# Retention and a gated MLP on one Trainium2 core: a weight load issued one instruction earlier, and a store and a load moved behind a later attention visit

## The chip, the core and the metric

The kernel runs on one core of a Trainium2 chip. The core has a matrix engine (TensorE; PE in the profile, with its weight loads as PEld), a vector engine (VectorE, DVE), a scalar engine (ScalarE, ACT), a general engine (GpSimd, POOL) and a sync engine (SyncE, SP) that issues transfers. Each runs its own list of instructions in order and waits on semaphores for the others. Transfers run on 16 DMA engines; those that POOL issues, and that change the type on the way, go by the software queue, those that SP issues by the hardware queues. The metric is the device time of one launch in microseconds (us): 291.16 us before, the median of 3 runs (291.06 to 291.24).

## The reference

Eight batches of eight heads, 576 positions, head size 64: scores masked by a decay that depends on the head and the distance, times v (no softmax). Its output, 4608 tokens of 512, goes through a two-layer MLP whose activation is h cos(h).

```python
scores = scale * np.matmul(q, k.transpose(0, 1, 3, 2))
Dmat = np.where(rel >= 0, gamma[:, None, None] ** rel[None, :, :], 0.0)
out = np.matmul(scores * Dmat[None], v)
x = np.ascontiguousarray(out.transpose(0, 2, 1, 3)).reshape(B * S, H * D)
h = x @ w_in                      # 512 -> 2048
return (h * np.cos(h)) @ w_out    # 2048 -> 512
```

## The kernel before

**Tiling.** Tokens are handled in 18 blocks of 256 (index j) for the attention and in 9 tiles of 512 (index n, two blocks each) for the MLP. The decay gamma^(i-j) is split into a factor for q's position and one for k's, so q and k are scaled row by row (`scaled`, L192: one instruction for each half y of a block), transposed by the matrix engine, multiplied to scores, masked (L312, L341), and multiplied by v (`out_own`, L433). What came earlier in a sequence enters by running state sums (`sums_of`, L351) and `out_carried` (L478), whose last matmul is kept as `tiles["end"]`. The result is cast to x, the first matrix's input. `mm1` (L520, matmuls at L534) makes h in eight groups a tile; ACT takes the cosine, DVE multiplies (L547, L548). `mm2_seven` (L670) makes the second product of a tile as seven products of half size, numbered x, in the order 1, 2, 6, 4, 7, 5, 3; their sums are the tile's four output quarters c11, c21, c22 and u1.

**The order.** The instructions of each engine stand in the order in which the program text emits them. In the opening (L899 to L948) the attention of blocks 0 and 1 is written out by hand between the loads of the weights. `load_w_in(e0, part)` (L812) has POOL issue a load of 512 columns of w_in; `part` 0 or 1 is the first or second half of the contraction. So w_in's first 512 columns come as piece one, `load_w_in(0, 0)`, and piece two, `load_w_in(0, 1)`; the next 512 as pieces three and four. The first group of h multiplies piece one for all its four parts, then block 1's attention output comes in between (`block1_outputs`, L979, with the casts of x at L984), then it multiplies piece two. Block 1's k is scaled by POOL in two halves (L920, L922), its q by DVE in two halves (L927); twelve transposes (L928 to L930, at L260) follow in the order q half 0, k half 1, q half 1, each group of four with its copy out of PSUM (L265) by DVE, ACT and DVE. POOL's casts of v (`round_v`, L933) and the other weight pieces follow.

**Later attention.** From the third tile on, two blocks' attention is visited between products: in the third tile (n = 2), a first visit ahead of product 7 (`mid_unit`, L1152) and a second ahead of product 3 (`end_unit`, L1165). Both call `outputs`, which ends with `out_carried` and so sets `tiles["end"]`.

**SP's queue.** SP issues all loads of q, k, v (`load`, L133; three buffers for each) and the stores of the outputs (`stored_rows`, L659, two DMAs for each quarter) in order. `store(...)` in `mm2_seven` decides when a finished quarter goes out; `late[x]` holds what is emitted right behind the visit ahead of product x. `gate=` makes the first DMA of a call wait for an instruction. The branch for n = 2 and the first quarter (s = 0, c11) is the one that changes. `loaded` is the next block to load; there it is 11.

Of the kernel before, what the change touches and what calls it, by code (L numbers as in the profile page):

```python
# [17 lines left out]
def kernel(  # L18
# [75 lines left out]
    tiles = {}  # L94
# [23 lines left out]
    def parts_of(t0, n, per):  # L118

        cut = -t0 % S  # L120
        if 0 < cut < n:
            return [(0, cut // per, t0), (cut // per, n // per, t0 + cut)]
        return [(0, n // per, t0)]
# [9 lines left out]
    def load(j, names="qkv", gate=None):  # L133
        for name in names:
            src = {"q": q, "k": k, "v": v}[name]
            if name == "q" or j < NP_B:
                f = ld.tile([P, H, 2, D], F32, tag="f" + name, name=f"f{name}")
                for p0, p1, t in parts_of(j * BK, BK, 2):
                    b, s0 = divmod(t, S)
                    i = nc.sync.dma_start(  # L140
                        f[p0:p1].rearrange("p h r d -> p h (r d)"),
                        src[b, :, s0 : s0 + 2 * (p1 - p0), :].rearrange(
                            "h (p r) d -> p h (r d)", r=2
                        ),
                    )
                    if gate is not None:
                        after(i, gate)
                        gate = None
            else:
                f = ld.tile([P, 2, H, D], F32, tag="f" + name, name=f"f{name}")  # L150
                for y in range(2):
                    for p0, p1, t in parts_of(j * BK + y * P, P, 1):
                        b, s0 = divmod(t, S)
                        i = nc.sync.dma_start(
                            f[p0:p1, y],
                            src[b, :, s0 : s0 + p1 - p0, :].rearrange("h s d -> s h d"),
                        )
                        if gate is not None:
                            after(i, gate)
                            gate = None  # L160
            tiles["f" + name, j] = f
        return i
# [90 lines left out]
    def transpose_pe(j, name, bank, evac, ys=(0, 1)):  # L253
        if ("qkT", j) not in tiles:
            new_qkT(j)
        m = "qk".index(name)
        ps = psum.tile([P, len(ys), HG, P], BF16, tag=bank, name="tr")
        for u, y in enumerate(ys):
            for hg in range(HG):
                nc.tensor.transpose(  # L260
                    ps[:, u, hg, :],
                    tiles["qks", j][:, m, y, hg].rearrange("s a d -> s (a d)"),
                    ident,
                )
        evac(tiles["qkT", j][:, m, ys[0] : ys[-1] + 1], ps)  # L265
# [404 lines left out]
    def mm2_seven(n, at, stored, xs=(1, 2, 6, 4, 7, 5, 3), early=None):  # L670
        pend = []

        def flush():
            while pend:
                pend.pop(0)()

        def add(out_, in0, in1):
            return lambda: nc.vector.tensor_tensor(out=out_, in0=in0, in1=in1, op=ALU.add)  # L678

        def copied(tag, x):  # L680
            t = op.tile([P, 2, N2], F32, tag=tag, name="ot")
            held.append(lambda ps=tiles["all", x]: nc.scalar.copy(t, ps))  # L682
            return t

        late = {4: [], 7: [], 3: []}

        def store(t, r, c, s):
            where = n * W + r * 256, c * N2, (c + 1) * N2, t

            def go():  # L690
                nonlocal loaded
                if 2 < n < last and s == 0:
                    stored_rows(*where, halves=(0,))
                    late[4].append(lambda: stored_rows(*where, halves=(1,), gate=tiles["end"]))
                    stored(s, late)
                elif n == 2 and s == 0:
                    step(False)

                    def behind(j=loaded):
                        stored_rows(*where, gate=tiles["end"])  # L700
                        load(j, "q")

                    late[7].append(behind)
                    late[3].append(lambda j=loaded: load(j, "kv", gate=tiles["end"]))
                    loaded += 1
                elif 1 < n < last - 1 and s == 1:
                    late[3].append(lambda: stored_rows(*where))
                else:
                    queues = (nc.sync, nc.scalar) if n == last and s else (nc.sync, nc.sync)
                    stored_rows(*where, queues)  # L710
                    stored(s)

            return go

        def copies():
            while held:
                held.pop(0)()

        for x in xs:
            if x not in at:  # L720
                copies()
                flush()
            else:
                if at[x].__name__ in ("nothing", "first_scores", "last_outputs", "turning"):
                    copies()
                at[x](flush, pend)
                copies()
                for run in late.pop(x, ()):
                    run()
            if x == 6 and n > 1:  # L730
                late_sums(n, (3,))
            parts = product(n, x, early)
            if x == 1:
                c11 = copied("a", 1)
                tiles["c11"] = c11
                if n > 1:
                    late_sums(n, (5, 6))
            elif x == 2:
                c11 = tiles["c11"]
                if n == 1:  # L740
                    p2 = copied("d", 2)
                    continue
                pend[:0] = [add(c11, c11, tiles["all", 2]), store(c11, 0, 0, 0)]
            elif x == 6:
                u1 = copied("b", 1)
            elif x == 4:
                c21 = copied("c", 4)
            elif x == 7 and n == 1:
                pend += [
                    add(c21, c21, tiles["all", 1]),  # L750
                    add(c22, c22, tiles["all", 1]),
                    store(c21, 1, 0, 1),
                    store(c22, 1, 1, 2),
                ]
            elif x == 7:
                c22 = copied("d", 1)
                pend += [add(c21, c21, tiles["all", 1]), store(c21, 1, 0, 1)]
            elif x == 5 and n == 1:
                c22 = copied("d", 5)
            elif x == 5 and n == last:  # L760
                for (j, c0, c1), ps in zip(parts, tiles["o", 5]):
                    pend.append(add(c22[:, j, c0:c1], ps, c22[:, j, c0:c1]))
                pend.append(store(c22, 1, 1, 2))
            elif x == 5:
                pend += [
                    add(c22, c22, tiles["all", 5]),
                    add(u1, u1, tiles["all", 5]),
                    store(c22, 1, 1, 2),
                ]
            elif n < last:  # L770
                pend += [add(u1, u1, tiles["all", 5 if n == 1 else 3]), store(u1, 0, 1, 3)]
                if n == 1:
                    pend += [add(c11, c11, p2), store(c11, 0, 0, 0)]
                flush()
            else:
                flush()
                copies()
                for (j, c0, c1), ps in zip(parts, tiles["o", 5]):
                    add(u1[:, j, c0:c1], ps, u1[:, j, c0:c1])()
                    if c1 == N2:  # L780
                        stored_rows(
                            n * W + j * P, N2, DM, u1[:, j : j + 1, :], (nc.sync, nc.scalar)
                        )

    loaded, prepared = 2, 0
# [26 lines left out]
    def load_w_in(e0, part=None):  # L812
        dgs = slice(0, DG) if part is None else slice(2 * part, 2 * part + 2)
        return nc.gpsimd.dma_start(  # L814
            w_in_sb[:, dgs, e0 : e0 + 512],
            moe_w_in[:, e0 : e0 + 512].rearrange("(dg p) e -> p dg e", p=P)[:, dgs],
        )
# [97 lines left out]
    w_dma = [load_w_in(0, 0)]  # L915
# [3 lines left out]
    sums_of(0, "st")()()  # L919
    scaled(nc.gpsimd, 1, "k", 0)  # L920
    transpose_pe(1, "k", "b", act, (0,))
    scaled(nc.gpsimd, 1, "k", 1)  # L922
    w_dma += [load_w_in(0, 1), load_w_in(512, 0)]
    ps0 = psum.tile([P, DG, BK], F32, tag="m", name="ov")
    out_own(0, ps0)
    for y in range(2):
# [287 lines left out]
```

## Time and profile before

| what | value |
|---|---|
| median of 3 runs | 291.16 us (291.06 to 291.24) |
| the profiled execution's own time | 291.54 us |
| its span, first to last instruction | 289.8 us |
| granted clock of the matrix engine, mean | 0.997 |
| chain that ended last: share of PE, of DMA | 92%, 4% |
| PE waiting for the load of w_in at L534 | 0.2 us, once |
| POOL waiting for the loads of v (L214), of k, of q (L203) | 6.8, 5.7 and 3.1 us |
| first group of h, first half; second half and all that follows | from 14.83; from 17.54 us |
| third tile: products from, to (fourth tile's h from) | 95.92, 111.86 us |

The span is what the profile covers; the time of a run has what lies around it too. Times inside the span count from its start. A row of the timeline merges neighbours of one line and form: start, length, engine, line, operation, out<-in, shapes, count, and in brackets the idle time before it and what ended it.

### The profile page before, as it was taken

How to read it: one execution, taken by the hardware profiler on the slowest of the kernel's cores; microseconds unless marked ns; L12 is line 12 of the kernel's file. 1: busy time of each engine (PE TensorE's matmuls, PEld its weight loads, DVE VectorE, ACT ScalarE, POOL GpSimd, SP SyncE). 2: the span in 40 equal slices, each digit the busy share in tenths (PEclk: the TensorE clock that was granted, in tenths of full speed). 3: DMA queues.
4: the chain of work that ended last, by engine and by line, in shares of the span. 5: the costliest groups of instructions: out<-in, count | busy, mean ns of one | idle time of the engine just before them, and what ended most of it. 6: DMA issues, size and time to landing. Idle time of an engine off the chain costs nothing.

```text
span 289.8 us, 10531 instructions
## 1 busy us (share of the span) xinstructions
PE 283.2 (98%) x4336; PEld 190.3 (66%) x4336; DVE 217.7 (75%) x311; ACT 169.5 (58%) x200; POOL 146.0 (50%) x169
## 2 busy tenths in 40 slices
PE   7999999999999999999999999999999999999994
PEld 2664446888844786478646874687458845874584
DVE  5767769969967977796789677977698669745943
ACT  6756316755677655677467747673767376536620
POOL 7940524786996993379236933594348023002300
PEclk9999999999999999999999999999999999999998
DMA  7999999997897897783883289317501120122013
GB/s 219 271 178 203 237 218 239 232 228 187 212 223 190 209 242 181 193 215 98 185 225 80 53 212 240 86 43 186 141 0 41 48 67 0 36 60 56 0 38 109
DMA packets 103853, 42.62 MB, mean 147 GB/s; under 512 B 68480, under 2 KB 103296, under 8 KB 103808
## 3 DMA queue, kind: packets, MB, share of 16 engines
q1 hardware_dynamic: 99104, 37.37, 52.6%
q0 software_dynamic: 4256, 4.19, 9.1%
q8 instruction: 36, 0.59, 0.9%
q10 hardware_dynamic: 448, 0.39, 0.4%
q14 instruction: 9, 0.07, 0.1%
HBM read 36.70 MB, written 9.44 MB: 159 GB/s over the span
## 4 chain that ended last, share of the span: by engine, by line
PE 92%; DMA 4%; POOL 1%; SPq 0%; issue 0%; ACT 0%; DVE 0%; POOLq 0%
PE h L534 43%; PE o L649 35%; PE o L1069 5%; PE tr L239 3%; PE ov L449 2%; DMA w_in_sb<-in_moe_w_in_dram 2%; DMA fv<-in_v_dram 2%; PE sc L332 2%; PE ov L484 1%; PE st L365 1%; POOL qks L203 1%; SPq L140 0%; POOL w_in_sb L814 0%; POOL vb L214 0%; ACT ot L682 0%
## 5 line engine op out<-in xcount | busy, mean ns | idle before, releaser
L534 PE MATMUL h<-xT,w_in_sb 128*128 128x512 bf16 (+1 forms) x656 | 127.8, 353 | 0.2 <-DMA w_in_sb<-in_moe_w_in_dram 0.2
L548 DVE TENSOR_TENSOR gT<-h,cosh 128x1024 bf16<-128x1024 f32 x72 | 87.8, 1221 | 28.2 <-ACT cosh L547 27.2
L547 ACT ACTIVATE cosh<-h,half_pi 128x1024 f32<-128x1024 f32 x72 | 80.1, 1114 | 39.5 <-PE h L534 39.5
L534 PEld LDWEIGHTS <-w_in_sb 128*128 128x128 bf16 x656 | 63.4, 98 | 59.3 <-issue 1.0
L588 POOL TENSOR_TENSOR gs<-gT 128x512 bf16<-128x512 bf16 x30 | 38.1, 1270 | 99.2 <-DVE gT L548 97.2
L649 PEld LDWEIGHTS <-gs 128*128 128x128 bf16 x528 | 49.6, 98 | 5.9
L203 POOL TENSOR_TENSOR qks<-fk,gkc 128x512 bf16<-128x512 f32 x32 | 38.5, 1222 | 5.7 <-DMA fk<-in_k_dram 5.7
L649 PEld LDWEIGHTS <-gT 128*128 128x128 bf16 x384 | 36.6, 98 | 6.1
L678 DVE TENSOR_TENSOR ot<-ot,o 128x512 f32<-128x512 f32 x35 | 23.3, 682 | 21.0 <-ACT ot L682 11.0
L245 ACT COPY qkT<-tr 128x1024 bf16<-128x1024 bf16 x28 | 26.8, 1022 | 13.0 <-PE tr L239 11.0
L203 POOL TENSOR_TENSOR qks<-fq,gq 128x512 bf16<-128x512 f32 x28 | 30.6, 1111 | 5.4 <-DMA fq<-in_q_dram 3.1
L649 PE MATMUL o<-w_out_sb,gs 128*128 128x256 bf16 (+1 forms) x264 | 30.7, 270 | 0.0
L649 PE MATMUL o<-w_out_sb,gT 128*128 128x256 bf16 x256 | 30.6, 273 | 0.0
L649 PE MATMUL o<-ws,gs 128*128 128x256 bf16 (+1 forms) x264 | 30.4, 269 | 0.0
L682 ACT COPY ot<-o 128x512 f32<-128x512 f32 x33 | 19.3, 584 | 19.1 <-PE o L649 19.1
L341 DVE TENSOR_TENSOR ret<-sc,mask_c 128x512 bf16<-128x512 f32 x32 | 20.6, 682 | 6.4 <-PE sc L332 6.4
L214 POOL CAST vb<-fv 128x512 bf16<-128x512 f32 x35 | 20.9, 621 | 6.9 <-DMA fv<-in_v_dram 6.8
L425 ACT CAST sb<-s_all 128x768 bf16<-128x768 f32 (+2 forms) x17 | 15.6, 919 | 14.6 <-DVE s_all L416 14.4
L416 DVE TENSOR_TENSOR s_all<-st,s_all 128x256 f32<-128x256 f32 x49 | 20.6, 421 | 1.4
L505 ACT CAST xT<-ov 128x1024 bf16<-128x1024 f32 (+1 forms) x16 | 15.2, 959 | 7.5 <-PE ov L484 7.4
L588 DVE TENSOR_TENSOR gs<-gT 128x512 bf16<-128x512 bf16 (+1 forms) x24 | 15.7, 654 | 0.5
L649 PE MATMUL o<-ws,gT 128*128 128x256 bf16 x128 | 15.3, 273 | 0.0
(85 smaller groups left out, 211.8 us busy)
## 6 DMA issues: line engine op xcount, KB each, us to landing
out_dram<-ot SPq DMA_DIRECT2D x68, 128.0 KB, 2.7
fk<-in_k_dram SPq DMA_DIRECT2D x28, 256.0 KB, 4.6
fv<-in_v_dram SPq DMA_DIRECT2D x28, 256.0 KB, 5.0
fq<-in_q_dram SPq DMA_DIRECT2D x12, 512.0 KB, 5.8
w_out_sb<-in_moe_w_out_dram POOLq DMA_DIRECT2D x4, 512.0 KB, 9.8
fq<-in_q_dram SPq DMA_DIRECT2D x4, 384.0 KB, 5.5
fk<-in_k_dram SPq DMA_DIRECT2D x2, 512.0 KB, 6.0
fv<-in_v_dram SPq DMA_DIRECT2D x2, 512.0 KB, 5.9
```

What stands on the lines that cost most here:

```text
L203: return eng.tensor_tensor(out=dst.rearrange("p b a d -> p a b d"), in0=src.rearrange("p (a b) d -> p a b d", a=2), in1=by.rearrange("p (a ...
L214: runs[y](vb[:, y], f[:, :, y, :] if j < NP_B else f[:, y])
L245: lambda r=r: evacs[r](tiles["qkT", j][:, :, :, :, r * HP : r * HP + HP], pss[r])
L341: nc.vector.tensor_tensor(out=ret[:, he].rearrange("p b y i -> p (b y) i"), in0=ps[he].rearrange("p b y i -> p (b y) i"), in1=mask_c.unsqu ...
L416: nc.vector.tensor_tensor(out=s32[:, u], in0=ps[c.half][:, c.y], in1=s32[:, u - 1] if u else tiles["run"], op=ALU.add,)
L534: nc.tensor.matmul(ps[:, j, :], lhsT=w_in_sb[:, dg, (et + j) * P : (et + j + 1) * P], rhs=xT[:, dg, c0 : c0 + w], start=dg == 0 and not (i ...
L547: nc.scalar.activation(cosh, ps, ACTF.Sin, bias=half_pi, scale=1.0)
L548: nc.vector.tensor_mul(gT[:, et : et + m, c0 : c0 + w], ps, cosh)
L588: i = eng.tensor_tensor(out=tiles["gs", n, x][:, e : e + step], in0=a[:, e : e + step], in1=b[:, e : e + step], op=op_,)
L649: nc.tensor.matmul(dst[i], lhsT=lhs[:, e, j * P : (j + 1) * P], rhs=rhs[:, e, c0:c1], start=(fresh and e == 0 and (i == 0 or len(parts) > 2)),
L678: return lambda: nc.vector.tensor_tensor(out=out_, in0=in0, in1=in1, op=ALU.add)
L682: held.append(lambda ps=tiles["all", x]: nc.scalar.copy(t, ps))
```

## The change

In the opening, the issue of piece two moves up by one instruction of POOL: between the two halves of block 1's k instead of behind both. Piece three stays behind the second half, and the list `w_dma`, by which later loads are gated, keeps its order.

In the third tile, the store of c11 and the load of q of block 11, so far emitted behind the visit ahead of product 7 (the store gated on that visit's last carried matmul), and the load of k and v, emitted behind the visit ahead of product 3 and gated on that one, become one step behind the visit ahead of product 3: store, gated on that visit's last carried matmul, then q, k and v. `load(j)` without names loads q, k, v in this order, without a gate of its own. SP's list there was: c11's two stores, q (two DMAs), c22's two stores, k (three), v (three), c21's stores. It becomes: c22's two stores, c11's two stores, q, k, v, c21's stores. The lists of the matrix, vector and scalar engines stay as they are.

```diff
-        late = {4: [], 7: [], 3: []}
+        late = {4: [], 3: []}
...
                     def behind(j=loaded):
                         stored_rows(*where, gate=tiles["end"])
-                        load(j, "q")
-
-                    late[7].append(behind)
-                    late[3].append(lambda j=loaded: load(j, "kv", gate=tiles["end"]))
+                        load(j)
+
+                    late[3].append(behind)
                     loaded += 1
...
     scaled(nc.gpsimd, 1, "k", 0)
     transpose_pe(1, "k", "b", act, (0,))
+    w_dma.append(load_w_in(0, 1))
     scaled(nc.gpsimd, 1, "k", 1)
-    w_dma += [load_w_in(0, 1), load_w_in(512, 0)]
+    w_dma.append(load_w_in(512, 0))
```

## The prediction

> **What bounds the kernel now.** I read the page's busy shares first, then the chain of waits, then the timeline of the opening, then single instructions where DVE and POOL meet, then SP's queue in the third tile.
>
> The page and the chain:
>
> ```profile
> PE 283.2 (98%) x4336; PEld 190.3 (66%) x4336; DVE 217.7 (75%) x311; ACT 169.5 (58%) x200; POOL 146.0 (50%) x169
> ...
> 9.44 1.99 POOL qks L203 x2
> 11.43 6.07 DMA w_in_sb<-in_moe_w_in_dram
> 17.54 13.15 PE h L534 x72
> ...
> 110.01 1.85 PE o L649 x16
> 111.86 13.81 PE h L534 x64
> ```
>
> The columns of the chain are start, length, what. TensorE is busy 98% of the span. From 17.54 us on the chain is PE nearly without a break; the third tile's end and the fourth's start (110.01 to 125.67) are PE only. Before 17.54 the chain is POOL's two scalings of k, then the landing at 17.49 of the second weight piece, which POOL issues behind them. So both edits touch something that reads well: the first shortens the one DMA wait on the chain, the second moves SP work in a stretch where SP is not on the chain.
>
> The timeline of the opening (start, length, engine, line, what, idle before it):
>
> ```profile
> 9.44 2.04 POOL L203 TENSOR_TENSOR qks<-fk,gkp 128x512 bf16<-128x512 f32 x2
> 11.24 1.39 DVE L203 TENSOR_TENSOR qks<-fq,gq 128x512 bf16<-128x512 f32 x2
> 11.43 1.47 POOL L814 DMA_DIRECT2D w_in_sb<-in_moe_w_in_dram  x2
> 12.15 0.93 PE L260 MATMUL tr<-ident,qks 128*128 128x128 bf16 x12
> 12.59 0.96 DVE L265 COPY qkT<-tr 128x512 bf16<-128x512 bf16 x2
> 13.60 0.64 PE L299 MATMUL sc<-qkT 64*64 64x128 bf16 x32
> 16.94 0.41 PE L484 MATMUL ov<-qkT,sb 64*64 64x128 bf16 x16
> 17.54 2.69 PE L534 MATMUL h<-xT,w_in_sb 128*128 128x256 bf16 x23 [0.20 <-DMA w_in_sb<-in_moe_w_in_dram]
> ```
>
> The last L484 matmul starts at 17.13 in the trace, and elsewhere a matmul follows an attention group 0.12 to 0.13 after it; so without the weights' wait h could start at 17.25. **That is all the first edit can win: 0.29 us.** The second thing to see is DVE: it works without a break from 8.84 to 13.55 (masks, q's two scalings at L203, two L265 copies), and the scores at 13.60 start 0.05 after the last copy. Here DVE sets PE, and any delay of DVE goes into PE one for one.
>
> **What POOL and DVE do to each other.** POOL's halves now run while DVE masks scores from PSUM, at 1.03 each. Single instructions elsewhere:
>
> ```profile
> 101.77 1.27 DVE L588 TENSOR_TENSOR gs<-gT,gs 128x2048 bf16<-128x2048 bf16 x1
> 101.92 2.02 POOL L203 TENSOR_TENSOR qks<-fk,gkc 128x512 bf16<-128x512 f32 x1
> ...
> 128.81 1.22 POOL L203 TENSOR_TENSOR qks<-fq,gq 128x512 bf16<-128x512 f32 x1
> 129.17 1.42 DVE L588 TENSOR_TENSOR gs<-gs,gT 128x1024 bf16<-128x1024 bf16 x1
> ...
> L203 DVE TENSOR_TENSOR qks<-fq,gq x2: 680/730/780, 11.2 to 11.9; 128x512 bf16<-128x512 f32 x2
> ```
>
> L588 reads both operands from SBUF. At 101.77 it starts first, POOL's scaling starts 0.15 later and lasts 2.02 in place of 1.04: it ends 0.90 after DVE's. At 129.17 POOL is first; DVE's instruction, 0.68 when alone, takes 1.42 and ends 0.55 after POOL's. So with two SBUF operands on DVE they take turns, a whole instruction at a time. With one operand in PSUM (L312, L341) both keep their length. DVE's scaling of q reads fq and gq, both in SBUF: its first half took 0.78, its second 0.68, and the first ended 0.55 after POOL's second half of k (12.025 against 11.473). It belongs to the kind that takes turns, and before it only just missed POOL.
>
> **First edit, step by step.** POOL's first half ends at 10.47. Now piece two is issued: POOL is busy 0.71 to 0.90 with one (ten issues of L814 and L820); I take 0.80, that of the w_out piece at 34.79, the issue that also follows scalings. It would start at 10.43 (POOL's records overlap by 0.03 to 0.05) and end at 11.23. The second half follows, 11.23 to 12.26 at 1.03: 0.79 later than 11.473, and over q's scaling by DVE, which is first due at 11.245 and not free of L312 before 11.33. POOL is ahead by a hair.
> - DVE's first q half ends 0.55 after POOL: 12.81 (before 12.03). Its second 0.605 later as before: 13.415.
> - q's last four transposes: 0.056 after it, at 13.47; their ends and the L265 copy keep their distances (12.686 to 13.546 before, 0.86): the copy ends at 14.33, the scores start at 14.385 against 13.599: **+0.786**.
> - If DVE is first instead, it ends at 11.93, POOL's half 0.90 later at 12.83, DVE's second half 0.55 later at 13.38: the scores at +0.75. The order of the two hardly matters. With issues of 0.71 and 0.90 the sum goes from +0.70 to +0.79.
> - From the scores to the last L484 everything waits on what was just made (ACT's x cast, masks, products): +0.786 stays. Last L484 at 17.91, h at 18.04, with the weights long there: against 17.537 that is **+0.50**. The 0.29 won is in this.
> - h's second block needs DVE's cast of x (L984, end 18.11 before, 18.90 now, 0.05 to PE). PE comes there after eight matmuls of 0.109, at 18.91: a wait of 0.03.
> - POOL's casts of v (0.62 each) now meet DVE's second q half and end some 0.4 later, 14.5; the state sums that read them start at 14.04+0.79 = 14.83. Hidden, with 0.3 left. The weight pieces behind them are issued 0.4 later; piece four landed at 20.35 and is needed at 21.03+0.5. Hidden by 1.2 at the old landing, 0.8 with the 0.4.
>
> [...]
>
> **Second edit.** The store of the first output quarter (two DMAs) and q's load of block 11 (two) go from behind product 7's visit to behind product 3's, after the two DMAs of the c22 store, and k and v (six) stay behind them. SP before:
>
> ```profile
> 106.34 2.67 SPq L665 DMA_DIRECT2D out_dram<-ot  x2
> 109.10 1.15 SPq L140 DMA_DIRECT2D fq<-in_q_dram  x2
> 110.34 2.62 SPq L665 DMA_DIRECT2D out_dram<-ot  x2
> 113.06 2.00 SPq L154 DMA_DIRECT2D fk<-in_k_dram  x3
> 115.16 2.19 SPq L154 DMA_DIRECT2D fv<-in_v_dram  x3
> ```
>
> SP is then busy until 126.19 and next needed at 131.21. The gate of the moved store is the last L484, 110.01. c22's store can go at 109.5, when its sum is made. Adding lengths: c22 2.6, c11 2.7, q 1.15, all before 116.0; k to 118.0, v to 120.2; the last load of block 12 is issued by 129.1. Landing takes 4.6 to 5.8 (the page): q(11) by 121.8, k(11) 122.6, v(11) 125.2. POOL uses them at 127.81, 130.00 and 132.89; block 12's at 134.01, 136.02, 138.00, landing by 130.6, 131.4, 134.1. **Cost 0**, cover 3.4 us at its smallest. Nothing to win either: PE has no gap there, and the stage's h (13.81) and products (3.60, 1.85) are as long in the later tiles. One DVE sum two tiles on waits for the moved store; it has 30 us.
>
> **Sum.** +0.50 +0.03 + 0 = +0.53 against the profiled 289.8 us (its run took 291.54, 0.38 over the median). PE has no later gap in which the delay would be lost, so the median goes from 291.16 to 291.7.
>
> **Rivals.**
> - *The wait just goes* (not slower). If POOL's half and DVE's ran side by side, q's transposes would be on time, k's (at 12.38) have 0.1 to spare over 12.26, and piece two, issued 1.0 earlier, lands at 16.5, before 17.25. h starts 0.29 sooner; the x cast (18.11+0.05 against 18.13) takes back 0.03. Then w_out's last piece lands at 42.23 and its first matmul starts at 42.32: unless it lands sooner too, all but 0.04 is lost. Gain 0.04 to 0.26, middle 291.0. It decides if DVE's q halves stay at 0.7. For it: L312 runs beside POOL untouched. Against: the three rows above.
> - *It does not do what it says.* No software-queue packet ran before 11.38, when the loads of q, k, v ended; if the second piece lands no sooner and nothing blocks: 291.16.
> - *The clock drops.* PE loses up to 0.8 us of work between 12.2 and 14.4. The page's clock is 9 to the last slice, through gaps of 0.4 at 15.9 and 17.3; the stretch after the end shows 0.5 for 3.65 us. If such a stretch came here, half of it is lost: +1.8, so 293.5.
> - *The late loads reach PE.* If each of the four stores took 2.0 to issue (the longest seen), q(11) would land at 124.5, still in time; the loads would need 3 us more. Each us beyond that is one on POOL, not yet on PE: 292 at most, an estimate from those slacks.
>
> **Chances and range.** Forecast 0.77, own range 291.5 to 292.0; the wait just goes 0.08; no effect 0.05; clock 0.06; late loads 0.02; 0.02 stays for a gain that I do not see. A measurement tells about 0.2%, 0.58 us, from no change: 291.74 is the line, and the forecast lies just under it; what I could not price (restarts of PE, a longer issue on POOL) only adds, so I put 0.6 of the forecast's chance above it. Slower 0.46 + 0.08 = 0.54; same 0.31 + 0.13 = 0.44; faster 0.02. The range 291.1 to 292.1 holds the forecast and no effect, and leaves out the clock and most of the gain.
>
> **What would show it.** In the profile after: DVE's L203 at 11.24 as a pair of about 2.2 us instead of 1.39; the scores near 14.4 instead of 13.60; h's long run near 18.0 with no DMA wait before it; POOL's second half between 11.2 and 12.3. SP: four stores before q's load, PE still whole from 110 to 126. Wrong would be: the pair still 1.4 long, or a DMA or POOL wait of PE after 100 us.

## The result and the profile after

The changed kernel takes 294.66 us, median of 7 runs (292.98 to 295.43), against 291.24 us (290.89 to 291.93, 7 runs) of the kernel before: a ratio of 1.0101, 95% interval 1.0070 to 1.0132. It is slower, as forecast, but by 3.4 us where 0.5 was forecast, and outside the range of 291.1 to 292.1.

The seven runs fall into two groups by their mean granted clock: 292.98, 293.07 and 293.55 us at 0.997 to 1.0, and 294.66 to 295.43 us at 0.987 to 0.991. So there are two losses, one of about 1.9 us in every run, and another of about 2.0 us in four of seven. The profiled execution (293.07 us, span 291.4, clock 0.997) is of the first group and shows the first loss alone.

The busy shares and the chain of waits of the kernel after (start, length, what):

```profile
PE 283.3 (97%) x4336; PEld 190.4 (65%) x4336; DVE 220.1 (76%) x311; ACT 169.6 (58%) x200; POOL 146.7 (50%) x169
```

```profile
8.86 2.49 DVE ret L312 x4
11.34 3.37 DVE qks L203 x2
...
19.42 13.09 PE h L534 x72
```

The wait for the second weight piece has left the chain, which was the aim of the first edit. DVE's two scalings of q stand in its place, at 3.37 us. DVE's total busy time is 2.4 us larger (220.1 against 217.7) with the same 311 instructions: it did not do more, it took longer.

The opening in the timeline of the kernel after (columns as before):

```profile
9.45 1.04 POOL L203 TENSOR_TENSOR qks<-fk,gkp 128x512 bf16<-128x512 f32 x1
10.44 0.76 POOL L813 DMA_DIRECT2D w_in_sb<-in_moe_w_in_dram  x1
11.22 1.06 POOL L203 TENSOR_TENSOR qks<-fk,gkp 128x512 bf16<-128x512 f32 x1
11.26 3.44 DVE L203 TENSOR_TENSOR qks<-fq,gq 128x512 bf16<-128x512 f32 x2
12.21 0.76 POOL L813 DMA_DIRECT2D w_in_sb<-in_moe_w_in_dram  x1
12.97 1.18 POOL L214 CAST vb<-fv 128x512 bf16<-128x512 f32 x2
14.62 0.41 DVE L265 COPY qkT<-tr 128x512 bf16<-128x512 bf16 x1
14.76 0.40 PE L260 MATMUL tr<-ident,qks 128*128 128x128 bf16 x4 [1.25 <-DVE qks L203]
15.67 0.64 PE L299 MATMUL sc<-qkT 64*64 64x128 bf16 x32
19.35 0.39 PE L534 MATMUL h<-xT,w_in_sb 128*128 128x256 bf16 x2
```

POOL's second half stands at 11.22 to 12.28, over DVE's first half. The pair of DVE's halves takes 3.44 where it took 1.39 and where 2.2 was forecast. The scores start at 15.67 (before 13.60, forecast 14.385), the second half of h's first group at 19.35 (before 17.54, forecast 18.04), with no wait for a transfer ahead of it: piece two landed at 15.99 instead of 17.49, 3.4 us before it was needed. The second and third tile start 1.8 us later (48.56 and 82.41 against 46.75 and 80.60), the fourth 1.6 (113.30 against 111.70).

A narrower window of the same timeline takes the second half apart:

```profile
12.76 1.94 DVE L203 TENSOR_TENSOR qks<-fq,gq 128x512 bf16<-128x512 f32 x1
...
12.97 0.62 POOL L214 CAST vb<-fv 128x512 bf16<-128x512 f32 x1
```

DVE's first half ends at 12.835, its second at 14.702. In between POOL casts v twice, each at its usual 0.62, until 14.150; DVE's half ends 0.55 after the second cast.

The four transfers of the second edit, SP's queue in the kernel after:

```profile
111.18 3.47 SPq L665 DMA_DIRECT2D out_dram<-ot  x4
114.75 1.07 SPq L140 DMA_DIRECT2D fq<-in_q_dram  x2
115.91 2.00 SPq L154 DMA_DIRECT2D fk<-in_k_dram  x3
118.00 2.63 SPq L154 DMA_DIRECT2D fv<-in_v_dram  x3
```

The order is the one forecast, everything is issued by 120.7, and the later tiles lose nothing against before (the end of the last matmuls is 1.6 us later, less than the 1.8 of h).

### The profile page after: what moved, and what is told of

It reads as the page before. It is cut to its first block, busy times and chain, and to the rows that moved or that the text cites. A ratio compares the mean times of both kernels' runs of the same rounds, so it can differ in the third digit from the quotient of the medians.

```text
span 291.4 us, 10533 instructions
## 1 busy us (share of the span) xinstructions
PE 283.3 (97%) x4336; PEld 190.4 (65%) x4336; DVE 220.1 (76%) x311; ACT 169.6 (58%) x200; POOL 146.7 (50%) x169
## 4 chain that ended last, share of the span: by engine, by line
PE 93%; DVE 4%; DMA 1%; issue 0%; ACT 0%; DVEq 0%
PE h L534 43%; PE o L649 34%; PE o L1069 5%; PE tr L239 3%; PE ov L449 3%; PE sc L332 2%; PE ov L484 2%; DVE ret L312 1%; PE st L365 1%; DMA fk<-in_k_dram 1%; DVE qks L203 1%; DVE qks L171 1%; PE sc L299 0%; ACT ot L682 0%; PE tr L260 0%
## 5 line engine op out<-in xcount | busy, mean ns | idle before, releaser
L214 POOL CAST vb<-fv 128x512 bf16<-128x512 f32 x35 | 21.8, 649 | 7.1 <-DMA fv<-in_v_dram 7.1
L588 DVE TENSOR_TENSOR gs<-gT 128x512 bf16<-128x512 bf16 (+1 forms) x24 | 16.3, 680 | 0.5
```

The costliest lines, as they stand in the source:

```text
L214: runs[y](vb[:, y], f[:, :, y, :] if j < NP_B else f[:, y])
L588: i = eng.tensor_tensor(out=tiles["gs", n, x][:, e : e + step], in0=a[:, e : e + step], in1=b[:, e : e + step], op=op_,)
```

## The experiments

All kernels in one table. "Scores" and "h" are the starts of block 1's scores and of the second half of h's first group in the profiled execution; "low" counts the runs with a mean clock of 0.994 or less. All other runs had 0.997 or more, called full clock below, and so had all 62 runs of the kernel before that were taken beside the experiments. Each ratio goes by the runs of the kernel before taken with it, whose medians lie between 291.09 and 291.29. A star marks a profile that itself holds a stretch of low clock, so its later times are not comparable.

| kernel | median us (runs) | ratio, 95% interval | scores | h | low |
|---|---|---|---|---|---|
| before | 291.24 (7) | 1 | 13.60 | 17.54 | 0 of 62 |
| after | 294.66 (7) | 1.0101, 1.0070 to 1.0132 | 15.67 | 19.35 | 4 of 7 |
| edit1_alone | 294.30 (6) | 1.0103, 1.0075 to 1.0132 | 16.04* | 20.37* | 5 of 6 |
| edit2_alone | 291.35 (12) | 1.0004, 0.9988 to 1.0020 | 13.57 | 17.31 | 0 of 12 |
| casts_behind_piece_four | 292.52 (12) | 1.0051, 1.0034 to 1.0069 | 15.33* | 20.51* | 4 of 12 |
| casts_on_act | 292.21 (10) | 1.0032, 1.0020 to 1.0045 | 14.32 | 18.00 | 2 of 10 |
| factors_in_psum | 291.81 (12) | 1.0019, 1.0005 to 1.0034 | 13.90 | 17.58 | 0 of 12 |
| factors_by_act | 291.75 (12) | 1.0016, 0.9998 to 1.0034 | 13.85 | 17.53 | 0 of 12 |
| warm_in_the_gap | 293.99 (6) | 1.0092, 1.0071 to 1.0113 | 15.67 | 19.35 | 3 of 6 |
| fillers_in_three_gaps | 293.74 (5) | 1.0093, 1.0080 to 1.0107 | 15.70 | 19.38 | 0 of 5 |
| pieces_ahead_of_k | 295.61 (4) | 1.0138, 1.0123 to 1.0152 | 13.63 | 20.91* | 4 of 4 |
| casts_at_once | 293.59 (1) | | 15.01* | 19.44* | 1 of 1 |
| one_cast_on_pool | 294.97 (1) | | 15.47* | 21.29* | 1 of 1 |
| cast_issue_cast | 295.17 (1) | | 16.00* | 21.26* | 1 of 1 |

### Which edit

**edit1_alone**: the kernel after with the second edit undone (the `late` lines as before).

> The weight piece between k's halves, and nothing of the second edit. Theory (the opening alone): DVE's second half of q's scaling again ends near 14.7, behind both of POOL's casts of v, the scores of block 1 start near 15.67, h's long run near 19.35, span 291.4 where the granted clock stays near 0.997; the time as with both edits, 293 to 295. Rival (the moved store and loads cost too): 1 us or more below that, span under 290.6.

**edit2_alone**: the kernel before with the second edit.

> The store and q's load behind the second visit, and the weight piece where it was before. Theory: PE is whole from 106 to 126, span 289.8 within 0.2, time as before (291.2). Rival (the second edit costs): a wait of PE or of POOL's scaling of blocks 11 and 12, time 0.6 us or more over before.

The first edit alone gives the whole loss, 1.0103, with DVE's second half ending at 14.75. The second alone gives 1.0004, nothing; its profiled span of 290.1 is 0.1 above what was expected, and PE has no gap over 0.25 us between 106 and 126. In that profile h starts 0.23 earlier than before, since piece two happened to land sooner (17.27), and then, its PE rows show, it is lost again:

```profile
42.52 0.81 PE L1068 MATMUL o<-w_out_sb,gT 128*128 128x512 bf16 x2 [0.30 <-DMA w_out_sb<-in_moe_w_out_dram]
```

PE comes early to w_out's last piece and waits for it; the kernel before started this run at 42.32. In this run the piece landed at 42.48, before at 42.23. So even a clean gain of the 0.29 us at stake in the first edit can be cut at this place.

### What holds DVE's second half

**casts_behind_piece_four**: the issue of piece four goes ahead of POOL's casts.

```diff
     act(x_of(0), ps0)
+    w_dma.append(load_w_in(512, 1))
     round_v(1)
-    w_dma += [load_w_in(512, 1), load_w_in(1024), load_w_in(1536)]
+    w_dma += [load_w_in(1024), load_w_in(1536)]
```

> Both edits, and POOL's two casts of v of block 1 moved behind the issue of piece four, so that two issues stand between k's second half and the casts. Theory (the casts took the turn of DVE's second half): that half ends near 13.4 in place of 14.70, the scores start near 14.4 in place of 15.67, h near 18.05 in place of 19.35, span near 290.3. Rival (POOL's transfer issues hold DVE off): the second half still ends later than 14, h after 18.7.

The timeline of casts_behind_piece_four:

```profile
12.20 1.48 POOL L813 DMA_DIRECT2D w_in_sb<-in_moe_w_in_dram  x2
12.75 1.09 DVE L203 TENSOR_TENSOR qks<-fq,gq 128x512 bf16<-128x512 f32 x1
...
13.67 1.19 POOL L214 CAST vb<-fv 128x512 bf16<-128x512 f32 x2
```

With the casts 0.7 later, DVE's second half ends at 13.84 instead of 14.70. At full clock the median is 292.43 (8 runs) where the kernel after has 293.07 (3 runs), 0.64 less; the medians of all runs lie 2.1 apart only because more of the runs after had a low clock. The half does not reach the expected 13.4, though POOL's first cast begins only at 13.67; the rival's bound of 14 is not reached either. This profile's clock is low from 13.2 on, so its scores and h decide nothing. By itself this run leaves open whether the casts or the issues hold the half; the next one settles it.

**casts_on_act**: both casts of v of block 1 go to ACT, ahead of its copy of k's second half; POOL keeps the transfer issues only.

```diff
     transpose_pe(1, "q", "a", vec, (0,))
+    round_v(1, (act, act))
     transpose_pe(1, "k", "st", act, (1,))
...
     act(x_of(0), ps0)
-    round_v(1)
```

> Both edits, with the two casts of v of block 1 done by ACT, ahead of its copy of k's second half, in place of POOL. Theory (DVE's second half lost its turn to POOL's casts): it ends near 13.4, the scores start near 14.4, h near 18.05; time 0.5 over before in runs with the full clock. Rival (transfer issues of POOL hold DVE off as well, seen as 0.4 us when two issues followed): it ends near 13.8, the scores start near 14.8, time 0.9 over before.

The timeline of casts_on_act:

```profile
12.13 1.47 POOL L813 DMA_DIRECT2D w_in_sb<-in_moe_w_in_dram  x2
12.29 1.14 ACT L214 CAST vb<-fv 128x512 bf16<-128x512 f32 x2
12.67 0.68 DVE L203 TENSOR_TENSOR qks<-fq,gq 128x512 bf16<-128x512 f32 x1
```

Here DVE's second half takes its 0.68 and ends at 13.35, beside ACT's casts and POOL's issues: with no cast on POOL the same issues cost it nothing. The scores start at 14.32 and h at 18.00, where the prediction had 14.385 and 18.04. Up to h this kernel does what the prediction had the changed kernel do. Its median, 292.21, is 0.9 over before; the eight runs at full clock have 292.13, still 0.8 over, where 0.5 was expected. Of that, 0.46 is h's delay. The profiled run, at 292.75 the slowest of the eight, lost another 0.8 by its end, all of it in the third tile, where 1.26 us lie between two of PE's matmul starts, 82.62 and 83.87 (0.31 at this place before). What PE waited for there the profile does not name. POOL's scaling of k and DVE's sums meet at this place, but in the kernel before they do so too and take as long (POOL's longer scaling 1.49, before 1.50). The other runs of this kernel have no profile, so what they lose beyond 0.46 is open.

**factors_in_psum**: the changed kernel, but DVE first copies q's 16 factors a row into PSUM, so that its scalings read one operand from SBUF and one from PSUM.

```diff
...
+    factors = psum.tile([P, 2, H], F32, tag="n", name="fac")
+    vec(factors, gq[:, 1])
     for y in range(2):
-        scaled(nc.vector, 1, "q", y)
+        scaled(nc.vector, 1, "q", y, factors)
```

> Both edits; DVE first copies the 16 factors of block 1's q into PSUM (one more instruction, 128x16) and then scales q with one operand in SBUF and one in PSUM. Theory (two operands in SBUF make DVE and POOL take turns): DVE's pair takes 1.4 in place of 3.4, the scores start within 0.3 of 13.60, h at 17.25 to 17.6 without a wait for weights, span 289.6 to 290.0, time near before or up to 0.3 under it. Rival (the turns come from something else, the f32 operands or the engine queues): the pair still takes over 2 us and h starts after 18.

The timeline of factors_in_psum (its lines count two more than in the kernel after):

```profile
11.30 1.05 POOL L205 TENSOR_TENSOR qks<-fk,gkp 128x512 bf16<-128x512 f32 x1
...
11.44 0.18 DVE L929 COPY fac<-gq 128x16 f32<-128x16 f32 x1
11.65 1.29 DVE L205 TENSOR_TENSOR qks<-fq,fac 128x512 bf16<-128x512 f32 x2
...
13.05 1.17 POOL L216 CAST vb<-fv 128x512 bf16<-128x512 f32 x2
```

The same two instructions on the same data take 0.69 and 0.68. The first runs wholly beside POOL's second half of k, beside which it took 1.57; the second now ends at 12.93, before the casts begin. So here the turns came with the second operand in SBUF: 1.57 with it, 0.69 without. The small copy and its place in the queue cost 0.3 us of the scores, and the time is 0.2% over before: the loss is nearly gone, and nothing is won. Why the median is 0.7 over its before, with h in the profile 0.04 late, was not seen.

**factors_by_act**: the same with the copy made by ACT, earlier, so that DVE has nothing more to do than before.

```diff
+    factors = psum.tile([P, 2, H], F32, tag="a", name="fac")
+    act(factors, gq[:, 1])
     sums_of(0, "st")()()
...
-    transpose_pe(1, "q", "a", vec, (0,))
+    transpose_pe(1, "q", "n", vec, (0,))
```

> The changed kernel with q's factors copied into PSUM as in the earlier run with factors in PSUM, but by ACT, ahead of its copy of the state sums (ACT is idle from 9.47 to 10.65), so that DVE has no instruction more than before; q's first transposes take another PSUM bank for that. Theory A (with one operand in PSUM nothing takes turns, and the 0.25 that the copy on DVE cost is gone): DVE's halves end at 12.02 and 12.62, scores 13.6, piece two lands near 16.05, h's second half at 17.25 to 17.35 without a wait for a transfer: the 0.29 that the edit could win at most, 0.15 to 0.3 under before in the span; time 290.9 to 291.3, which the measurement will hardly tell from before (ratio 0.999 to 1.001). Theory B (something else keeps h late, DVE's cast of x or w_out's last piece): 291.3 to 291.8.

DVE's halves end at 11.96 and 12.56, as early as expected, and take 0.69 and 0.68 although POOL's second half of k runs beside both. But in the profiled execution the load of block 1's k landed at 9.68 (9.29 before), POOL's second half of k ended at 12.66, and now k's transposes set the scores, 13.85; whether the other runs had the late load was not seen. The median is 291.75, ratio 1.0016 (0.9998 to 1.0034). It does not beat the kernel before; of all kernels tried none does.

### In which order they take turns

**casts_at_once**: no transfer issue between POOL's second half of k and the casts; piece three follows behind them.

```diff
-    w_dma.append(load_w_in(512, 0))
...
-    w_dma += [load_w_in(512, 1), load_w_in(1024), load_w_in(1536)]
+    w_dma += [load_w_in(512, 0), load_w_in(512, 1), load_w_in(1024), load_w_in(1536)]
```

> Both edits, and POOL's two casts of v directly behind k's second half; the issue of piece three follows them. Theory A (strict turns, the longest waiting first): k's half ends at 12.28, DVE's first half 12.83, one cast 13.45, DVE's second half 14.0, then the other cast; the scores start near 15.0. Theory B (POOL goes on with the next instruction whenever it has one that reads SBUF and DVE has to come between by luck): both casts run before DVE's second half, which ends near 14.1 to 14.2 after casts that end 13.6, or DVE's first half waits as well.

The timeline of casts_at_once:

```profile
12.30 1.99 POOL L214 CAST vb<-fv 128x512 bf16<-128x512 f32 x2
12.72 1.10 DVE L203 TENSOR_TENSOR qks<-fq,gq 128x512 bf16<-128x512 f32 x1
```

Here they alternate: POOL's k half ends at 12.24, DVE's first half at 12.80, POOL's first cast at 13.27, DVE's second half at 13.82, POOL's second cast at 14.29. Now the casts are delayed too, to 0.97 and 1.07 from 0.62. So alternation exists, and the kernel after departs from it.

**one_cast_on_pool**: the kernel after with the second cast on ACT (`round_v(1, (nc.gpsimd.tensor_copy, act))`).

> The changed kernel, with the second of POOL's two casts of v given to ACT. Open is why DVE's second half of q's scaling waited for both casts (12.835 to 14.702), when without a transfer issue ahead of them casts and halves alternated. Theory A (a POOL instruction that reads SBUF goes ahead of DVE's waiting one whenever it follows a POOL instruction without a gap; DVE has its turn 0.55 after the last of such a row): the one cast ends at 13.60 and DVE's half at 14.15, scores near 15.12. Theory B (the wait is one of the transfer issue's, 1.2 us whatever stands behind): the half ends at 14.70 as in the changed kernel. Theory C (the casts do not matter, DVE's half is only 0.6 behind the first): 13.4.

**cast_issue_cast**: the issue of piece four between the two casts.

> The changed kernel, with the issue of piece four moved between POOL's two casts of v: issue of piece three, cast, issue of piece four, cast. Theory A (casts that stand back to back keep DVE out together; an issue between them lets it in): first cast at 12.97 to 13.60, DVE's second half of q ends at 14.15, the second cast at 14.3 to 14.9. Theory B (any cast that is still queued on POOL goes first): the half ends 0.55 after the second cast, near 15.45, scores past 16.4. Time: A 293.0 to 293.4, B 294.2 or more, each at a granted clock of 0.997 or above.

The timelines of one_cast_on_pool and then of cast_issue_cast:

```profile
12.75 1.39 DVE L203 TENSOR_TENSOR qks<-fq,gq 128x512 bf16<-128x512 f32 x1
...
12.96 0.62 POOL L214 CAST vb<-fv 128x512 bf16<-128x512 f32 x1
```

```profile
12.76 1.74 DVE L203 TENSOR_TENSOR qks<-fq,gq 128x512 bf16<-128x512 f32 x1
12.97 0.62 POOL L214 CAST vb<-fv 128x512 bf16<-128x512 f32 x1
13.53 0.71 POOL L815 DMA_DIRECT2D w_in_sb<-in_moe_w_in_dram  x1
14.24 0.72 POOL L214 CAST vb<-fv 128x512 bf16<-128x512 f32 x1
```

With one cast the half ends at 14.137, 0.556 after the cast, as theory A said: the second cast in the kernel after is worth the other 0.56. With an issue between the casts it ends at 14.503, which neither theory gave (14.15 or 15.45): later than one cast explains, and before the second cast is done. The times of these two single runs, at a clock of 0.988, decide nothing.

### The clock

The rows below are stretches of 3 us: start and end, length, then busy time (and count) of PE, PEld, DVE, ACT and POOL, the granted clock, the share of the transfer engines and their GB/s. First the kernel before, then after, then casts_behind_piece_four:

```profile
12.00:15.00 3.00, 3.00 (x103) 2.31 (x92) 2.16 (x5) 2.56 (x4) 3.00 (x6) 1.00 0.97 142
```

```profile
12.00:15.00 3.00, 1.10 (x28) 0.75 (x19) 3.00 (x3) 0.97 (x2) 3.00 (x6) 1.00 1.19 184
15.00:18.00 3.00, 2.91 (x84) 2.18 (x82) 2.12 (x4) 1.95 (x2) 2.79 (x4) 1.00 0.92 128
```

```profile
12.00:15.00 3.00, 2.01 (x36) 1.25 (x29) 2.60 (x4) 1.09 (x3) 3.00 (x6) 0.70 1.20 192
15.00:18.00 3.00, 2.67 (x68) 2.35 (x69) 1.56 (x2) 1.94 (x2) 2.80 (x4) 0.50 1.20 189
18.00:21.00 3.00, 2.89 (x59) 1.92 (x58) 1.68 (x5) 0.79 (x2) 0.00 (x0) 0.66 1.23 201
```

Before, PE is busy all the time between 12 and 15 us. After, it is busy for 1.10 of 3 us. In this execution of the kernel after the clock stays at 1.00 through it; in the profiled one of casts_behind_piece_four it falls to 0.5 from 13.2 on, for 6.83 us, and the run took 294.15 us where eight others of that kernel took 292.19 to 292.83. In edit1_alone it fell for 3.41 us, from 15.18. One stretch of 3.41 us at half clock lowers the mean over the span by 0.006 (3.41 × 0.5 / 291), two by 0.012: that fits the runs at 0.993 or 0.994 (the profiled one of edit1_alone has 0.993) and at 0.987 or 0.988 (that of casts_behind_piece_four 0.988).

**warm_in_the_gap**: six filler matmuls on zeros ahead of q's last four transposes, where PE waits (`warm(6, "n")`).

> Both edits, and six matmuls on zeros (128x512, 0.216 each at full clock, 1.3 us together) between k's transposes and q's last four, where PE stood idle from 13.3 to 14.76. They change nothing that is computed. Theory (the runs above 294 are those in which the granted clock fell to 0.5 for one or two stretches of 3.4 us after PE had stood half idle between 12.2 and 15.7): no run has a mean clock under 0.995, all lie within 0.5 us of the lowest, near 293.1, the scores start at 15.7 as before. Rival (the slow runs have another cause, chips or transfers): half of the runs are above 294 as before.

**fillers_in_three_gaps**: the same six there, and four more ahead of q's first transposes.

> The changed kernel with ten more filler matmuls (on zeros): four ahead of q's first transposes (PE idle from about 12.0 to 12.9) and six ahead of q's last four (13.2 to 14.76). With six fillers in the second gap alone the lowest clocks of the runs (0.987 to 0.991) were gone, but three of six runs still showed 0.993 or 0.994. Theory A (the clock falls because PE is half idle there, the first gap counting too): no run under 0.997, median 293.0 to 293.6, ratio 1.006 to 1.008. Theory B (the fall comes from the later gaps, 15.3 to 17, or is not tied to idle time): still runs near 0.993 or 0.994 and a median over 293.8. The scores stay at 15.67 by both.

With six fillers three of six runs still had a clock of 0.993 or 0.994; with ten no run of five was under 0.998. The stretch of fillers_in_three_gaps:

```profile
12.00:15.00 3.00, 2.84 (x37) 1.66 (x30) 3.00 (x3) 0.98 (x2) 3.00 (x6) 1.00 1.20 182
```

PE's busy time between 12 and 15 us is 2.84 where it was 1.10 (2.30 with six fillers). In these runs the low clock went with the idle PE. The other kernels agree, as far as their profiles are at full clock: with 2.55 us or more of 3 (before, edit2_alone, both kernels with factors in PSUM, ten fillers) none of 103 runs had a low clock, with 2.30 or less (after, casts_on_act, six fillers) 9 of 23 had. In the opening the fillers change nothing else: scores 15.70, h 19.38. But 293.74 us are left, 0.9% over before and 0.1 above the range expected. The fastest runs with ten fillers, 293.35 and 293.50, are no faster than the runs of the kernel after at full clock, and one took 294.43 at a clock of 1.0. So with the low clock gone the median came down by 0.9 us, not by the whole 2.0; what the slower of these runs lost was not seen.

### Another way to send the pieces early

**pieces_ahead_of_k**: k's halves stay where they were, and pieces one and two are both issued early, ahead of them and of the state sums.

```diff
+    w_dma = [load_w_in(0, 0)]
     round_v(0, (nc.gpsimd.tensor_copy, act))
-    w_dma = [load_w_in(0, 0)]
+    w_dma.append(load_w_in(0, 1))
...
     scaled(nc.gpsimd, 1, "k", 1)
-    w_dma += [load_w_in(0, 1), load_w_in(512, 0)]
+    w_dma.append(load_w_in(512, 0))
```

> The kernel before, with piece one issued ahead of POOL's cast of v of block 0, in the 1.1 us in which POOL waits for that v (6.69 to 7.79), and piece two behind this cast; both halves of k stay where they were, beside DVE's masks. The order of the rest is that of before. Theory (the DMA wait at 17.54 can go if POOL's halves stay out of DVE's way): piece two lands by 16.5, DVE's pair takes 1.4, the scores start at 13.6, h at 17.25 to 17.3; span 0.1 to 0.3 under before, time 290.8 to 291.0. Rival (the earlier pieces take bandwidth from the loads of q and v of block 1): q's scaling starts later than 11.3 and the time is equal or worse.

The timeline of pieces_ahead_of_k:

```profile
11.34 1.32 DVE L203 TENSOR_TENSOR qks<-fq,gq 128x512 bf16<-128x512 f32 x2
...
13.63 0.64 PE L299 MATMUL sc<-qkT 64*64 64x128 bf16 x32 [0.28 <-DVE qkT L265]
...
15.32 1.63 POOL L214 CAST vb<-fv 128x512 bf16<-128x512 f32 x2 [3.10 <-DMA fv<-in_v_dram]
...
15.98 0.22 PE L382 MATMUL st<-vb,qks 64*64 64x64 bf16 x2 [1.71 <-POOL vb L214]
```

DVE's pair takes 1.32 and the scores are on time at 13.63: without POOL's scaling beside it nothing is lost there. But v of block 1 landed at 15.26 instead of 12.29, POOL's casts wait 3.1 us for it and PE for the casts. It is the slowest kernel of all, 1.0138, and all four runs had a low clock too. So the earlier issue of the pieces came with a load, needed by the next step, that landed 2.97 us later.

## Why the prediction was right or wrong

**Right: the mechanism.** In this opening DVE and POOL took turns where DVE read both operands from SBUF: its first half took 1.57 beside POOL's second half of k. In factors_in_psum, without the second SBUF operand, it took 0.69 beside the same instruction. POOL was ahead by a hair (11.22 to 11.26), and DVE's first half ended 0.56 after it: 12.835, forecast 12.81.

A half that waited for the last POOL instruction ended 0.55 to 0.56 after it, in every run where it could be read (after, casts_at_once, one_cast_on_pool); where nothing of POOL's held it, it took 0.68 (casts_on_act).

**Wrong: "Its second 0.605 later as before: 13.415."** This is the step that failed. It measured 1.87 later, 14.702. The prediction had seen that POOL's casts of v meet this half, and gave the turn to DVE: "POOL's casts of v (0.62 each) now meet DVE's second q half and end some 0.4 later ... Hidden". It was the other way round: the casts kept their 0.62, and the half stood behind both. That step was priced only for the side that was hidden, POOL's; the side on the path, DVE's, should have had a bound from above. The forecast had k's second half to 12.26; the rows of before have 0.72 for the issue of piece three, 1.17 for both casts and 0.55 from POOL's end to DVE's; together 14.70. One_cast_on_pool shows one cast's worth (14.137), casts_on_act none (13.351).

**Right: the rest of the chain.** From the end of the second half to the scores the prediction had 0.97; it measured 0.969. The 1.29 that the failed step was short, added to the forecast h of 18.04, gives 19.33; it measured 19.35. Added to 291.7 it gives 293.0; the three runs at full clock took 292.98 to 293.55. So what the first loss has beyond the forecast is this one term. And casts_on_act, where the term is as forecast, has scores and h within 0.07 of the forecast. Its time is not as near: 0.8 over its before at full clock where the forecast had 0.5, so that the step from h to the end of the run has 0.3 us open. The forecast had no later gap in which a delay is lost; in the profile after, 0.2 of the 1.8 us are made up again by the fourth tile.

**Right: what the first edit could win.** The scores moved by 2.07, h by 1.81: the 0.26 between them is the wait for piece two, forecast as at most 0.29.

**Right: the second edit costs nothing** (edit2_alone 1.0004), and w_out's last piece takes back a gain of h, as the rival "the wait just goes" had it; that rival itself fell with the 3.4 us of DVE's pair.

**Wrong: the chance of the clock.** It had 0.06, and came in 4 of 7 runs. It was priced for a PE that loses up to 0.8 us of work between 12.2 and 14.4; with the half 1.29 later PE lost 1.9 us of 3. But it also fell in 2 of 10 runs of casts_on_act, whose scores are where the forecast had them. So 0.06 was low even for the forecast. The price, +1.8 for one stretch, came near the 2.0 us between the two groups by luck: by their mean clocks, 0.987, 0.988, 0.988 and 0.991, those runs mostly had two stretches. Runs with the mean clock of one stretch took about 1.1 us more (edit1_alone 294.06 and 294.07 against 292.95, casts_on_act 293.26 against 292.13). What decides which executions fall was not shown.

## What to carry to other kernels

When an instruction is moved beside another that shares a resource with it, price the turns for both engines and for everything queued behind, the one on the path from above: every neighbour may go first. Here VectorE's scalings of q, on the path and with both inputs in SBUF, took 1.57 and 1.87 us next to GpSimd's scaling and casts; with the small operand put into PSUM they took 0.69 and 0.68 next to the same scaling (factors_by_act). And where TensorE worked for only 1.10 of 3 us, 4 of 7 runs had a mean clock of 0.987 to 0.991 and took about 2.0 us more than the other three, so it pays to read several runs with their clocks before believing one profile.

## What was not expected of the hardware

**Who goes next.** DVE's first half ended at 12.75 to 12.84 in all these runs. The second ended 0.60 later in casts_on_act, where no cast of POOL's came in.

| POOL's list behind k's second half | DVE's second half ends |
|---|---|
| issue, issue, issue (casts_on_act) | 13.35 |
| cast, cast (casts_at_once) | 13.82, alternating |
| issue, issue, cast, cast (casts_behind_piece_four) | 13.84 |
| issue, cast, issue, issue (one_cast_on_pool) | 14.14, after the cast |
| issue, cast, issue, cast (cast_issue_cast) | 14.50 |
| issue, cast, cast (after) | 14.70, after both casts |

In these runs issues with no cast behind them cost DVE nothing (0.68 in casts_on_act). A cast behind a single issue went ahead of a half that had been waiting since before it (the half ended 0.556 after the cast in one_cast_on_pool), and a second cast right behind it went too (0.55 after that one in the kernel after); without the issue they alternated, and behind two issues the half ended 0.17 after the first cast began. And in the third and the fifth row the half ended some 0.4 us later than the instructions that overlap it explain; in both an issue was running with a cast queued behind it. Why is open. The rows bear this much: here the order of turns could not be read off the start times, and the upper bound, all of POOL's readers first, was reached (14.70).

**The clock fell only in part of the executions** of one kernel, to 0.5 for 3.41 us (edit1_alone) or 6.83 us (casts_behind_piece_four), and the falls went with the idle time of PE between 12 and 18 us: never in 62 runs of the kernel before, in 4 of 7 after, in none of 5 with the gaps filled. The idle time ahead of a fall was not always long: in casts_behind_piece_four the clock fell at 13.2, and the longest gap of PE in the six us ahead was 0.61 us.

**A hardware-queue load landed 2.97 us later when a software-queue issue behind it came earlier.** In pieces_ahead_of_k SP's issue of v of block 1 began at 6.33, POOL's of pieces one and two at 6.74 and 8.49 (before 8.40 and 11.43), and v landed at 15.26 instead of 12.29. The software queue's first packet ran at 9.95, while the hardware queue's loads were still running; before it was 11.38.
